# Two-phase blocks: a second MLP whose second products also go by Strassen's scheme

## The chip, the cores and the metric

The kernel runs on one core of a Trainium2 chip. The metric is the device time of one execution in microseconds (us); smaller is better. TensorE does the matmuls, VectorE (DVE) and ScalarE (ACT) work on elements, GpSimd (POOL) only issues the stores here, and SyncE (SP) only issues the loads. All transfers run on the core's 16 DMA engines.

## What is computed

A retention layer (a linear attention with decay) over q, k and v gives 3072 tokens of 512 features. Two MLPs follow, each with a hidden width of 2048:

```python
def _moe_ref(x, w_in, w_out):      # first MLP, "layer 0"
    h = x @ w_in
    g = np.maximum(0.01 * h, h)
    return (g @ w_out).astype(np.float32)

def _moe2_ref(x, w_in, w_out):     # second MLP, "layer 1"
    h = np.maximum(x @ w_in, 0.0)
    return (h * h @ w_out).astype(np.float32)
```

## The kernel before

Each MLP runs over three blocks of 1024 tokens (`b`), and a block has two halves of 512 tokens (`t`). Every matrix operand is split into a high and a low float32r part, and a product is three matmuls: high by high, low by high, high by low. The matmul is always 128x128 weights by 128x512 moving values. The hidden width is worked through in eight steps `q`, each with two 128-wide columns `j = 2q, 2q + 1`.

**First product.** In all blocks but the very first it goes by Strassen's scheme (in Winograd's form). For a step `q`, `emit_in` forms seven products of six matmuls, 42 in place of 48. Seven combinations of the weights ("units") are made once by `make_in` (`load_w`, `cast`, four subtractions, two splits), stored to DRAM (`wid`) and read again by `read_in`. Seven combinations of the tokens come from `operands` and lie in the tiles `xh1` to `xl7`.

**Second product.** It is plain: `emit_out` does 12 matmuls for one `j` and one half `t` (four output columns `m`, three passes). The weights come from `make_out` in the first block of a layer, which stores them to `wod`, and from `read_out` after that. A block has two passes. In the q loop the first product of step `q` alternates with `put_out` (second product, `t = 0`) of step `q - 1`; the hidden values of `t = 1` are kept in `t0` to `t7`. Then a second pass over the 16 `j` does the second product of `t = 1` in the order `LATE`: `split_late` splits the kept values, `read_out` brings the weights through the two buffers of the tile `wo`, and `operands` makes the next block's token combinations. So a block of layer 1 has 336 + 384 = 720 matmuls.

**Order.** Matmuls, loads and stores are kept in the order of the program. Loads form one queue on SP and stores one on POOL, and an issue that waits for its buffer holds back all behind it. ACT's and DVE's instructions are ordered when the program is built, by a planner that estimates when each becomes ready; on the chip each engine then goes strictly by that order.

**Work done ahead.** During the last block of layer 0 (`lay == 0`, `b == 2`), `make_in(1, 0, ..., True)` makes the first-product units of layer 1 for the steps in `AHEAD`, one after q = 1, 3, 5 and 7, through the tiles `ea` and `eb`. The others are made in layer 1's block 0, where raw weights come through the tile `sg` (`load_w`, 1 MiB each).

Of the kernel before, what the change touches and what calls it, by code (L numbers as in the profile page):

```python
# [9 lines left out]
F32 = mybir.dt.float32  # L10
F32R = mybir.dt.float32r
# [47 lines left out]
):  # L59
    nc = tc.nc  # L60
    x_p = ctx.enter_context(tc.tile_pool(name="x", bufs=1))
    w_p = ctx.enter_context(tc.tile_pool(name="w", bufs=1))
    g_p = ctx.enter_context(tc.tile_pool(name="g", bufs=2))
# [9 lines left out]

    def swap_pools():
        early.close()
        late["p"] = ctx.enter_context(tc.tile_pool(name="late", bufs=1))

    qt = const.tile([P, NP, C], F32, name="qt")
    vt = const.tile([P, NP, 2, 2], F32, name="vt")
# [10 lines left out]
    def store(**io):  # L90
        tc.keep_in_program_order(nc.gpsimd.dma_start(**io))
# [128 lines left out]


    wid = {}
    wod = {}
# [11 lines left out]
    stage = {}  # L235

    def load_w(lay, q, half):
        t = stage[lay, q, half] = w_p.tile([P, 1024], U64, tag="sg", name="sg", bufs=2)
        load(out=t, in_=src[lay][q, half])

    def cast(s, r):
# [71 lines left out]
    def get_in(lay, b, q):  # L313
        if lay == 0 and b == 0:
            plain_in(q)
        elif (lay == 0 and b == 1) or (lay == 1 and b == 0 and q not in AHEAD):
            make_in(lay, b, q)
        else:
            read_in(lay, b, q)

    def make_out(lay, q):
        load_w(lay, q, 1)
        if lay == 0 and 0 < q < NQ - 1:
            f = g_p.tile([P, 2, T], F32, tag=f"t{NQ - 1}", name="of", bufs=1).rearrange("p j c -> p (j c)")
        else:
            f = w_p.tile([P, 1024], F32, tag="wf", name="of", bufs=1)
        cast(stage.pop((lay, q, 1)), f)
        o = w_p.tile([P, 2, 2, 512], F32R, tag="wo", name="wo", bufs=2)
        fv = f.rearrange("p (j c) -> p j c", j=2)
        nc.scalar.copy(o[:, 0], fv)  # L330
        nc.vector.tensor_tensor(out=o[:, 1], in0=fv, in1=o[:, 0].bitcast(F32), op=ALU.subtract)
        store(out=wod[lay, q], in_=o.rearrange("p l j c -> p (l j c)").bitcast(F32))
        wout[lay, q] = o

    def read_out(lay, q):
        o = w_p.tile([P, 2, 2, 512], F32R, tag="wo", name="wo", bufs=2)
        load(out=o.rearrange("p l j c -> p (l j c)").bitcast(F32), in_=wod[lay, q])
        wout[lay, q] = o


# [47 lines left out]

    def keep(ps, t=None):
        if t is None:  # L390
            t = g_p.tile([P, T], F32, tag="g", name="g", bufs=3)
        nc.scalar.copy(t, ps)  # L392
        return t

# [9 lines left out]
    def emit_in(lay, b, q):  # L404

        j0, j1 = 2 * q, 2 * q + 1
        pa = ps_h.tile([P, T], F32, tag="h", name="pa")
        product(lay, b, q, 1, pa, True, True)
        c11 = g0[j0] = keep(pa)
        pd = ps_h.tile([P, T], F32, tag="h", name="pd")  # L410
        product(lay, b, q, 5, pd, True, True)
        late_g[q] = g_p.tile([P, 2, T], F32, tag=f"t{q}", name="g", bufs=1)
        c22 = g1[j1] = keep(pd, late_g[q][:, 1])
        yield
        product(lay, b, q, 6, pa, False, True)
# [15 lines left out]
        g = g0[j1] = g_p.tile([P, T], F32, tag="g", name="g", bufs=3)  # L431
# [12 lines left out]
    def emit_plain(q, i, t):  # L444
        j = 2 * q + i
        a = win[0, q]
        ps = ps_h.tile([P, T], F32, tag="h", name="pa")
        for kb in range(KB):
            kh, kt = divmod(kb, 2)
            unit = 2 * (1 - kh) + i if kh == 0 else 1 - i  # L450
            for k, (l, r) in enumerate(((0, 0), (1, 0), (0, 1))):
                mm(
                    out=ps, lhsT=a[:, l, unit, kt * P:(kt + 1) * P], rhs=xop[t, kh][r][:, kt],
                    start=kb == 0 and k == 0, stop=kb == KB - 1 and k == 2,
                )
        if t == 0:
            g = g_p.tile([P, T], F32, tag="g", name="g", bufs=3)
# [17 lines left out]
    def split_g(g, tag=None):  # L475
        if tag:
            gg = g_p.tile([P, 2, T], F32R, tag=tag, name="gg", bufs=1)
            gh, gl = gg[:, 0], gg[:, 1]
        else:
            gh = g_p.tile([P, T], F32R, tag="gh", name="gh")  # L480
            gl = g_p.tile([P, T], F32R, tag="gl", name="gl")
        mark[0] = nc.scalar.copy(gh, g).ins  # L482
        mark[1] = nc.vector.tensor_tensor(out=gl, in0=g, in1=gh.bitcast(F32), op=ALU.subtract).ins  # L483
        return gh, gl

    def emit_out(lay, b, t, j, part=(0, 12), begin=False, end=False):
# [10 lines left out]
        for k, m in order[part[0]:part[1]]:  # L497
            l, r = passes[k]
            mm(
                out=ac[m], lhsT=o[:, l, j % 2, m * P:(m + 1) * P], rhs=r,  # L500
                start=begin and k == 0, stop=end and k == 2,
            )
        if part[1] == 12:
# [18 lines left out]

    zero = g_p.tile([P, T], F32R, tag="gh", name="zero")
# [40 lines left out]

    for lay in range(2):
        for b in range(NB):
            last = lay == 1 and b == NB - 1
            if not last:  # L570
                nl, nb = (lay, b + 1) if b + 1 < NB else (1, 0)
            rest = (b + 2) * B * NP if lay == 0 and b + 1 < NB else 0
            for q in range(NQ):
# [11 lines left out]
                else:  # L585
# [12 lines left out]
                    for _ in part:  # L598
                        pass
                if q + 1 < NQ:  # L600
                    get_in(lay, b, q + 1)
                    get_out(lay, b, q + 1)
                elif not last:
                    get_in(nl, nb, 0)
                if not last and nl and q == 2:
# [12 lines left out]
            for i in range(NJ):  # L618
# [4 lines left out]
                    read_out(lay, LATE[i // 2 + 2])  # L623
                if rest and i < 9:
                    attend(rest)
                if not last:
# [5 lines left out]
                if not last and i == 13:  # L632
                    get_out(nl, nb, 0)
            evacuate(lay, b, 1)
            if (lay, b) == (0, NB - 2):
                swap_pools()


_OUT = ((NB, P, KB, TB), "float32")
# [62 lines left out]
```

## Time and profile before

| | |
|---|---|
| median of 3 runs | 1161.13 us (1159.62 to 1161.87) |
| the profiled execution: its own time | 1160.83 us |
| the profiled execution: its span, first to last instruction | 1158.8 us |
| TensorE busy | 1133.4 us (98%), 5402 matmuls |
| weight loads busy | 891.9 us (77%) |
| VectorE / ScalarE busy | 587.6 us (51%) / 508.2 us (44%) |
| granted TensorE clock, mean | 0.995 |

Times are microseconds from the first instruction. Matmul durations in the trace overlap, since matmuls are pipelined; the distance from one start to the next is the cost of one. Layer 0's last block runs from 484 to 659 us, layer 1's block 0 from there to 828, its block 1 to 991 and its block 2 to the end.

### The profile page before, as it was taken

The numbers are of one execution on the slowest core, as the hardware profiler recorded it, in microseconds if no ns is written. First come the engines' busy times: TensorE is split into PE (matmuls) and PEld (weight loads), VectorE is DVE, ScalarE is ACT, GpSimd is POOL, SyncE is SP. The second block draws the span as 40 slices with busy tenths as digits, with TensorE's granted clock in tenths as the row PEclk, the third lists the DMA queues.
The fourth block names the chain that finished last, engine by engine and source line by source line (L and its number), as shares of the span: only waits on it lengthen the run. The fifth ranks groups of instructions, "written<-read, shape, count | busy, mean of one in ns | idle before, by whom it ended". The sixth has DMA issues, their size and how long they took to land.

```text
span 1158.8 us, 13722 instructions
## 1 busy us (share of the span) xinstructions
PE 1133.4 (98%) x5402; PEld 891.9 (77%) x5402; DVE 587.6 (51%) x852; ACT 508.2 (44%) x793; POOL 54.2 (5%) x104
## 2 busy tenths in 40 slices
PE   8999999999999999999989999999999999999998
PEld 5677777767777776788867877788888888888886
DVE  5866555665444353442556477877232355233341
ACT  3755453323343342343445366755333353333431
POOL 0000000001000000000001000000000000000000
PEclk9999999999999999999999999999999999999999
DMA  9565654548455444749755788854746435645334
GB/s 373 234 245 201 234 202 150 186 140 291 184 211 218 167 169 164 254 191 371 300 200 209 300 314 321 318 198 181 297 158 258 184 143 195 239 197 200 136 126 165
DMA packets 48800, 255.71 MB, mean 221 GB/s; under 512 B 5984, under 2 KB 8032, under 8 KB 27872
## 3 DMA queue, kind: packets, MB, share of 16 engines
q1 hardware_dynamic: 36576, 192.04, 44.8%
q0 software_dynamic: 11584, 61.87, 13.5%
q8 instruction: 43, 0.70, 0.3%
q10 hardware_dynamic: 576, 0.93, 0.2%
q14 instruction: 21, 0.17, 0.0%
HBM read 191.90 MB, written 62.91 MB: 220 GB/s over the span
## 4 chain that ended last, share of the span: by engine, by line
PE 85%; DMA 9%; DVE 3%; ACT 2%; issue 1%; ACTq 0%; SPq 0%; DVEq 0%
PE acc L85 42%; PE pa L85 23%; PE pd L85 8%; DMA sg<-w 4%; PE y L85 4%; PE pb L85 4%; PE sc L85 3%; DMA wa<-wid 1%; DMA wo<-wod 1%; PE sp L85 1%; DMA gt<-gtab 1%; DVE of L248 1%; DMA wf<-wraw 1%; ACT sg L246 0%; DVE of L251 0%
## 5 line engine op out<-in xcount | busy, mean ns | idle before, releaser
L85 PE MATMUL acc<-gh,wo 128*128 128x512 f32 x1200 | 315.4, 394 | 9.8 <-ACT gh L482 6.0
L85 PEld LDWEIGHTS acc<-gh,wo 128*128 128x128 f32 x1200 | 225.5, 189 | 61.4 <-ACT gh L482 8.9
L85 PE MATMUL pa<-xh,wa 128*128 128x512 f32 x576 | 181.2, 395 | 2.3 <-DVE wa L272 1.4
L85 PE MATMUL acc<-gl,wo 128*128 128x512 f32 x600 | 169.3, 389 | 0.1
L483 DVE TENSOR_TENSOR gl<-g,gh 128x512 fp32r<-128x512 f32 x150 | 101.6, 688 | 77.6 <-PE acc L85 55.1
L85 PEld LDWEIGHTS acc<-gl,wo 128*128 128x128 f32 x600 | 112.6, 188 | 24.1 <-DVE gl L483 0.6
L85 PEld LDWEIGHTS pa<-xh,wa 128*128 128x128 f32 x576 | 106.2, 188 | 28.7 <-ACT g L462 2.3
L85 PE MATMUL acc<-gg,wo 128*128 128x512 f32 x504 | 122.1, 391 | 0.0
L482 ACT CAST gh<-g 128x512 fp32r<-128x512 f32 x150 | 91.2, 620 | 67.6 <-PE acc L85 66.8
L85 PE MATMUL pa<-xl,wa 128*128 128x512 f32 x288 | 112.5, 391 | 0.3 <-DVE xl L348 0.3
L85 PEld LDWEIGHTS acc<-gg,wo 128*128 128x128 f32 x504 | 94.0, 188 | 20.0 <-issue 0.7
L85 PE MATMUL pa<-xh,wb 128*128 128x512 f32 x320 | 99.6, 393 | 0.5 <-ACT g L392 0.5
L85 PE MATMUL pd<-xh,wa 128*128 128x512 f32 x320 | 98.7, 390 | 0.0
L418 DVE TENSOR_TENSOR g<-g,pd 128x512 f32<-128x512 f32 x40 | 27.5, 687 | 130.5 <-PE pd L85 122.7
L392 ACT COPY g<-pa 128x512 f32<-128x512 f32 x80 | 46.9, 587 | 98.5 <-PE pa L85 98.4
L85 PEld LDWEIGHTS pa<-xh,wb 128*128 128x128 f32 x320 | 59.4, 188 | 15.4 <-issue 1.7
L85 PEld LDWEIGHTS pd<-xh,wa 128*128 128x128 f32 x320 | 60.0, 188 | 12.7 <-ACT g L392 0.2
L149 DVE TENSOR_TENSOR pm<-sc,mk 128x384 f32<-128x384 f32 x96 | 49.2, 551 | 33.1 <-PE sc L85 30.8
L397 ACT ACTIVATE g<-g 128x512 f32<-128x512 f32 x48 | 30.2, 631 | 79.0 <-DVE g L422 31.8
L85 PEld LDWEIGHTS pa<-xl,wa 128*128 128x128 f32 x288 | 54.0, 188 | 12.3 <-DVE xl L348 0.7
L85 PE MATMUL pa<-xl,wb 128*128 128x512 f32 x160 | 62.3, 389 | 0.0
L85 PE MATMUL pd<-xl,wa 128*128 128x512 f32 x160 | 62.3, 389 | 0.0
(79 smaller groups left out, 1250.0 us busy)
## 6 DMA issues: line engine op xcount, KB each, us to landing
wo<-wod SPq DMA_DIRECT2D x68, 1024.0 KB, 4.8
sg<-w SPq DMA_DIRECT2D x32, 1024.0 KB, 7.7
wa<-wid SPq DMA_DIRECT2D x28, 1024.0 KB, 7.0
wb<-wid SPq DMA_DIRECT2D x28, 768.0 KB, 6.7
wod<-wo POOLq DMA_DIRECT2D x16, 1024.0 KB, 5.4
r<-first SPq DMA_DIRECT2D x48, 256.0 KB, 3.4
wid<-wa POOLq DMA_DIRECT2D x12, 1024.0 KB, 4.2
wid<-wb POOLq DMA_DIRECT2D x12, 768.0 KB, 5.7
```

What stands on the lines that cost most here:

```text
L85: tc.keep_in_program_order(nc.tensor.matmul(**kw))
L149: nc.vector.tensor_tensor(out=t, in0=sc[h][:, 128:512], in1=mk[:, p, h], op=ALU.mult)
L248: nc.vector.scalar_tensor_tensor(out=ru, in0=hi, scalar=0x80000000, in1=ru, op0=ALU.bitwise_and, op1=ALU.bitwise_or,)
L392: nc.scalar.copy(t, ps)
L397: nc.scalar.activation(out=g, in_=g, func=AF.Lrelu)
L418: nc.vector.tensor_tensor(out=c12, in0=c12, in1=pd, op=ALU.add)
L482: mark[0] = nc.scalar.copy(gh, g).ins
L483: mark[1] = nc.vector.tensor_tensor(out=gl, in0=g, in1=gh.bitcast(F32), op=ALU.subtract).ins
```

## The change

Layer 1's blocks 1 and 2 are taken out of the common loop and done by a new function, `both_block`, in two phases.

Phase 1 (`first_half`, `second_half`) forms the first products of all eight steps, the seven products of step `n` alternating with those of step `n - 1`. All hidden values are kept: `gu` (tiles `u0` to `u7`) and `gt_` (tiles `t0` to `t7`).

Phase 2 does the second product by the same scheme, with the hidden columns' parity, the output halves and the token halves as the two-by-two blocks. It has seven stages, in the order `STAGES`; each is one product over all eight `q` and two `m`, 48 matmuls, 336 in all. `prepare` forms and splits the next stage's hidden combination while a stage runs. `read_stage` reads a stage's weight units, four loads of 512 KiB, into tiles of the token combinations (or `t0` to `t7`) that are free by then.

The units of the second weights are eight in number and lie in one DRAM tensor per layer, `wou`: for each partition, unit, step, part and 256 columns. Units 0 to 3 are the plain quarters, written by `make_out` (also in layer 0, in place of `wod`); units 4 to 7 are made by the new `out_combinations` from a raw copy (`wraw`): for steps 0 and 1 in layer 1's block 0 during the pass for `t = 1`, for steps 2 to 7 in phase 1 of block 1. `read_out` now reads four pieces of 2 KiB per partition where it read 8 KiB in one.

Around this: weights and temporaries move to other memory pools, and layer 1's pool is exchanged for a new one (`swap_left`, `swap_right`) during its block 0; `AHEAD` has five steps, made after q = 0, 1, 2, 4 and 6; in layer 1's block 0 the raw weights are requested before `get_in`, every third through an additional `sg` buffer, and `read_x` comes at q = 4.

```diff
-AHEAD = (0, 1, 3, 5)
+AHEAD = {0: 0, 1: 1, 3: 2, 5: 4, 6: 6}
+OUNIT = {1: 0, 2: 2, 4: 3, 7: 4, 5: 5, 3: 6, 6: 7}
+STAGES = (1, 5, 6, 3, 7, 2, 4)
...
+    def swap_left():
+        mid.close()
+        late["p"] = ctx.enter_context(tc.tile_pool(name="units", bufs=1, reuse_waits="tile"))
...
-            wod[lay, q] = dram.tile([P, 2 * 1024], F32, name=f"wod{lay}_{q}")
+    wou = [dram.tile([P, 8 if lay else 4, NQ, 2, 256], F32, name=f"wou{lay}") for lay in range(2)]
...
+        pool, bufs = (late["p"], 1) if late and n_stage[0] % 3 == 0 else (w_p, 2)
+        t = stage[lay, q, half] = pool.tile([P, 1024], U64, tag="sg", name="sg", bufs=bufs)
...
-        store(out=wod[lay, q], in_=o.rearrange("p l j c -> p (l j c)").bitcast(F32))
+        put_units(lay, q, 0, o)
         wout[lay, q] = o
+        if lay:
+            store(out=wraw[q], in_=f)
+    def out_combinations(q, f, ta, tb):
+        load(out=f, in_=wraw[q])
+        yield
+        a11, a21, a12, a22 = (f[:, n * 256:n * 256 + 256] for n in range(4))
+        tt = nc.vector.tensor_tensor
+        tt(out=a11, in0=a11, in1=a21, op=ALU.subtract)
+        tt(out=a21, in0=a21, in1=a22, op=ALU.add)
+        tt(out=a22, in0=a22, in1=a11, op=ALU.subtract)
+        tt(out=a12, in0=a12, in1=a22, op=ALU.subtract)
+        for n, t in ((0, ta), (2, tb)):
+            u = t.bitcast(F32R).rearrange("p (n l c) -> p n l c", n=2, l=2)
+            h = f[:, n * 256:(n + 2) * 256].rearrange("p (n c) -> p n c", n=2)
+            nc.scalar.copy(u[:, :, 0], h)
+            nc.vector.tensor_tensor(out=u[:, :, 1], in0=h, in1=u[:, :, 0].bitcast(F32), op=ALU.subtract)
+            store(
+                out=wou[1][:, 4 + n:6 + n, q].rearrange("p n l c -> p n (l c)"),
+                in_=t.rearrange("p (n c) -> p n c", n=2),
+            )
     def read_out(lay, q):
+        load(
+            out=o.bitcast(F32).rearrange("p n l c -> p n (l c)"),
+            in_=wou[lay][:, 0:4, q].rearrange("p n l c -> p n (l c)"),
+        )
...
+    def read_stage(n, ks):
+        i = STAGES[n]
+        for k in ks:
...
+            load(out=t.bitcast(F32), in_=wou[1][:, OUNIT[i], 2 * k:2 * k + 2])
+            units[i, k] = t
+    def split_rot(i, q, s):
+        r = late["r"].tile([P, 2, T], F32R, tag="rot", name="rot", bufs=NQ)
+        mark[0] = nc.scalar.copy(r[:, 0], s).ins
+        mark[1] = nc.vector.tensor_tensor(out=r[:, 1], in0=s, in1=r[:, 0].bitcast(F32), op=ALU.subtract).ins
+        rot[i, q] = r
+    def first_half(b, q):
...
+        product(1, b, q, 1, pa, True, True)
+        nc.scalar.copy(u[:, 0], pa)
+        yield
+        product(1, b, q, 5, pd, True, True)
+        nc.scalar.copy(t[:, 1], pd)
+        yield
+        product(1, b, q, 6, pa, False, True)
+        nc.scalar.copy(t[:, 0], pa)
+        yield
+        product(1, b, q, 3, pd, False, True)
+        nc.vector.tensor_tensor(out=t[:, 0], in0=t[:, 0], in1=pd, op=ALU.add)
+        act_sbuf(1, t[:, 0], True)
+        yield pa
+    def second_half(b, q, pa):
...
+        product(1, b, q, 7, pa, False, True)
+        nc.vector.tensor_tensor(out=t[:, 1], in0=t[:, 1], in1=pa, op=ALU.add)
+        act_sbuf(1, t[:, 1], True)
+        yield
...
+        product(1, b, q, 2, pb, True, True)
+        nc.vector.tensor_tensor(out=u[:, 0], in0=u[:, 0], in1=pb, op=ALU.add)
+        act_sbuf(1, u[:, 0], False)
+        split_rot(1, q, u[:, 0])
+        nc.vector.tensor_tensor(out=u[:, 0], in0=t[:, 0], in1=u[:, 0], op=ALU.subtract)
+        nc.vector.tensor_tensor(out=t[:, 0], in0=t[:, 1], in1=t[:, 0], op=ALU.subtract)
+        yield
+        product(1, b, q, 4, pa, False, True)
+        nc.scalar.activation(out=u[:, 1], in_=pa, func=AF.Relu)
+        nc.vector.scalar_tensor_tensor(out=u[:, 1], in0=pa, scalar=0.0, in1=u[:, 1], op0=ALU.max, op1=ALU.mult)
+        yield
+    def prepare(i, q):
...
+        elif i == 6:
+            nc.vector.tensor_tensor(out=u[:, 0], in0=t[:, 1], in1=u[:, 0], op=ALU.subtract)
+            split_rot(i, q, u[:, 0])
...
+    def both_block(b):
...
+        for n in range(NQ + 1):
+            f = first_half(b, n) if n < NQ else iter(())
+            r = second_half(b, n - 1, pa) if n else iter(())
+            for k in range(4):
+                pa = next(f, None)
+                if n == NQ - 1 and k < 2:
+                    read_stage(0, (2 * k, 2 * k + 1))
+                if k < 3:
+                    next(r, None)
+            if n == NQ - 1:
+                read_stage(1, range(4))
+            if n and n + 1 < NQ:
+                read_units(b, n + 1)
...
+        for n, i in enumerate(STAGES):
...
+                if e % 2 and n + 1 < len(STAGES):
+                    prepare(STAGES[n + 1], q)
+                if e == 1:
+                    if 1 <= n <= 5:
+                        read_stage(n + 1, range(4))
+                    if n == 1 and not last:
+                        read_x(b + 1)
+                    if n in (3, 5) and not last:
+                        read_units(b + 1, (n - 3) // 2)
...
     for lay in range(2):
         for b in range(NB):
+            if lay and b:
+                both_block(b)
+                continue
...
+                    if lay:
+                        load_w(lay, q + 1, 1)
+                        if q + 1 not in AHEAD.values():
+                            load_w(lay, q + 1, 0)
...
-                if lay == 0 and b == NB - 1 and q % 2:
-                    make_in(1, 0, AHEAD[q // 2], True)
+                if lay == 0 and b == NB - 1 and q in AHEAD:
+                    make_in(1, 0, AHEAD[q], True)
...
+            if lay:
+                swap_left()
+                read_units(1, 0)
+                made = [out_combinations(e, *scratch(*(f"u{7 - 3 * e - k}" for k in range(3)))) for e in range(2)]
+                for m in made:
+                    next(m)
```

## Rows read from the trace of the kernel before

**Rows 1.** Stretches: us; busy (and instructions) of each engine; PE clock, DMA share, GB/s.

```profile
664.00:776.00 112.00, 109.28 (x473) 87.93 (x472) 89.20 (x117) 78.78 (x112) 10.53 (x20) 1.00 0.80 306
776.00:828.00 52.00, 52.00 (x230) 42.77 (x230) 27.53 (x34) 20.40 (x30) 3.33 (x7) 1.00 0.48 175
828.00:991.00 163.00, 163.00 (x720) 134.82 (x719) 63.56 (x87) 66.29 (x107) 4.05 (x8) 1.00 0.54 206
991.00:1154.50 163.50, 163.22 (x721) 134.73 (x719) 51.88 (x77) 59.65 (x100) 3.46 (x7) 1.00 0.46 174
```

**Rows 2.** The chain that ended last: start us, us, what.

```profile
827.68 1.36 PE pa L85 x6
...
991.00 1.36 PE pa L85 x6
...
1014.12 2.72 PE pa L85 x12
...
1154.26 0.69 DVE y L519
```

**Rows 3.** PE's waits, 460 to 830 us: total us, times, longest.

```profile
PE acc L85 <- ACT gh L482: 6.0, 5, 4.7
PE acc L85 <- DMA wo<-wod: 3.8, 2, 2.5
PE pa L85 <- DVE wa L272: 0.8, 1, 0.8
PE pa L85 <- DMA wa<-wid: 0.6, 1, 0.6
PE pa L85 <- ACT g L392: 0.5, 1, 0.5
```

**Rows 4.** The chain in layer 0's last block.

```profile
522.06 17.34 DMA wa<-wid
...
585.10 15.01 DMA sg<-w
...
604.36 12.52 PE acc L85 x48
...
616.89 7.82 DMA wo<-wod
...
624.84 34.23 PE acc L85 x144
```

**Rows 5.** The same columns as rows 1, around that place and two DMA-bound stretches.

```profile
524.50:539.50 15.00, 14.42 (x65) 11.62 (x63) 3.36 (x5) 5.76 (x12) 0.50 (x1) 1.00 1.01 399
585.00:604.40 19.40, 14.69 (x66) 11.86 (x64) 6.30 (x8) 8.51 (x15) 0.55 (x2) 0.98 0.69 269
604.40:606.90 2.50, 2.50 (x6) 2.02 (x7) 2.47 (x6) 1.16 (x2) 0.00 (x0) 0.50 0.00 0
690.00:705.00 15.00, 14.82 (x65) 11.93 (x65) 9.53 (x12) 8.82 (x13) 1.07 (x2) 1.00 1.01 416
```

**Rows 6.** Timelines of SP and ACT: start us, us, engine, line, operation.

```profile
521.63 0.38 SPq L88 DMA_DIRECT2D xs<-ydr  x1
522.06 0.42 SPq L88 DMA_DIRECT2D wa<-wid  x1
...
600.13 1.12 ACT L245 ACTIVATE wf<-sg 128x1024 f32<-128x1024 f32 x1 [5.82 <-DMA sg<-w]
...
789.40 33.19 SPq L88 DMA_DIRECT2D wo<-wod  x7
```

**Rows 7.** DMA issues: out<-in, engine, count, KB each, median us to landing.

```profile
wo<-wod SPq DMA_DIRECT2D x68, 1024.0 KB, 4.8
...
r<-first SPq DMA_DIRECT2D x48, 256.0 KB, 3.4
```

**Rows 8.** DVE and ACT groups: shapes, count, busy us, mean ns of one, idle before.

```profile
L483 DVE TENSOR_TENSOR gl<-g,gh 128x512 fp32r<-128x512 f32 x150 | 101.6, 688 | 77.6 <-PE acc L85 55.1 <-ACT gh L482 22.0
L418 DVE TENSOR_TENSOR g<-g,pd 128x512 f32<-128x512 f32 x40 | 27.5, 687 | 130.5 <-PE pd L85 122.7 <-ACT g L392 7.9
L402 DVE SCALAR_TENSOR_TENSOR g<-g 128x512 f32<-128x512 f32 x24 | 16.6, 690 | 0.7
L291 DVE TENSOR_TENSOR wf<-wf 128x256 f32<-128x256 f32 x16 | 6.8, 423 | 18.4 <-DMA wf<-wraw 18.3
L482 ACT CAST gh<-g 128x512 fp32r<-128x512 f32 x150 | 91.2, 620 | 67.6 <-PE acc L85 66.8 <-DVE g L436 0.4
L392 ACT COPY g<-pa 128x512 f32<-128x512 f32 x80 | 46.9, 587 | 98.5 <-PE pa L85 98.4
L399 ACT ACTIVATE g<-g 128x512 f32<-128x512 f32 x48 | 30.2, 630 | 49.3 <-DVE g L418 31.1 <-DVE g L422 18.1
```

More of the change, by code (lines that the diff above doesn't have):

```diff
@@ L234, in retention_then_two_mlps @@
     src = (w1, w2)
-    stage = {}
+    stage, n_stage = {}, [0]
     def load_w(lay, q, half):
-        t = stage[lay, q, half] = w_p.tile([P, 1024], U64, tag="sg", name="sg", bufs=2)
+        if (lay, q, half) in stage:
+            return
+        n_stage[0] += 1
+        pool, bufs = (late["p"], 1) if late and n_stage[0] % 3 == 0 else (w_p, 2)
+        t = stage[lay, q, half] = pool.tile([P, 1024], U64, tag="sg", name="sg", bufs=bufs)
         load(out=t, in_=src[lay][q, half])
@@ L315, in get_in @@
             plain_in(q)
-        elif (lay == 0 and b == 1) or (lay == 1 and b == 0 and q not in AHEAD):
+        elif (lay == 0 and b == 1) or (lay == 1 and b == 0 and q not in AHEAD.values()):
             make_in(lay, b, q)
@@ L324, in make_out @@
             f = g_p.tile([P, 2, T], F32, tag=f"t{NQ - 1}", name="of", bufs=1).rearrange("p j c -> p (j c)")
+        elif lay and q:
+            f = late["p"].tile([P, 1024], F32, tag=("ea", "eb")[q % 2], name="of")
         else:
@@ L327, in make_out @@
         cast(stage.pop((lay, q, 1)), f)
[L328 to L331, printed above, removed]
-        store(out=wod[lay, q], in_=o.rearrange("p l j c -> p (l j c)").bitcast(F32))
-        wout[lay, q] = o
-    def read_out(lay, q):
-        o = w_p.tile([P, 2, 2, 512], F32R, tag="wo", name="wo", bufs=2)
-        load(out=o.rearrange("p l j c -> p (l j c)").bitcast(F32), in_=wod[lay, q])
+        o = o_p.tile([P, 4, 2, 256], F32R, tag="wo", name="wo", bufs=2)
@@ new lines, in scratch, with put_units @@
+    def scratch(*tags):
+        out = []
+        for t in tags:
+            p = late["r"] if t == "ss" else g_p if t[0] == "t" else late["p"]
+            out.append(p.tile([P, 2, T], F32, tag=t, name="of", bufs=2 if t == "ss" else 1).rearrange("p i c -> p (i c)"))
+        return out
+    def put_units(lay, q, n, t):
+        store(
+            out=wou[lay][:, n:n + 4, q].rearrange("p n l c -> p n (l c)"),
+            in_=t.bitcast(F32).rearrange("p n l c -> p n (l c)"),
+        )
+    def read_out(lay, q):
+        o = o_p.tile([P, 4, 2, 256], F32R, tag="wo", name="wo", bufs=2)
+        load(
+            out=o.bitcast(F32).rearrange("p n l c -> p n (l c)"),
+            in_=wou[lay][:, 0:4, q].rearrange("p n l c -> p n (l c)"),
+        )
@@ L499, in emit_out @@
             mm(
-                out=ac[m], lhsT=o[:, l, j % 2, m * P:(m + 1) * P], rhs=r,
+                out=ac[m], lhsT=o[:, 2 * (j % 2) + m // 2, l, m % 2 * P:(m % 2 + 1) * P], rhs=r,
                 start=begin and k == 0, stop=end and k == 2,
@@ L521, in evacuate, with read_units @@
             put(out=dst[:, m, t * T:(t + 1) * T], in_=y)
-    zero = g_p.tile([P, T], F32R, tag="gh", name="zero")
+    gu, gt_, units, rot = {}, {}, {}, {}
+    def read_units(b, q):
+        a = late["p"].tile([P, 2, 4, 256], F32R, tag="wa", name="wa", bufs=2)
+        c = late["p"].tile([P, 2, 3, 256], F32R, tag="wb", name="wb", bufs=2)
+        load(out=a.rearrange("p l n c -> p (l n c)").bitcast(F32), in_=wid[1, q][:, 0:2048])
+        load(out=c.rearrange("p l n c -> p (l n c)").bitcast(F32), in_=wid[1, q][:, 2048:3584])
+        put_in(1, q, a, c)
@@ new lines, in split_rot @@
+    def split_rot(i, q, s):
[4 more added lines that the diff above has]
+    def first_half(b, q):
+        u = gu[q] = late["p"].tile([P, 2, T], F32, tag=f"u{q}", name="gu")
+        t = gt_[q] = g_p.tile([P, 2, T], F32, tag=f"t{q}", name="gt")
+        pa = ps_h.tile([P, T], F32, tag="h", name="pa")
+        pd = ps_acc.tile([P, T], F32, tag=f"acc{2 + q % 2}", name="pd")
+        product(1, b, q, 1, pa, True, True)
[11 more added lines that the diff above has]
+        yield pa
@@ new lines, in prepare @@
+    def prepare(i, q):
+        u, t = gu[q], gt_[q]
+        if i == 5:
+            split_rot(i, q, u[:, 0])
+        elif i == 6:
+            nc.vector.tensor_tensor(out=u[:, 0], in0=t[:, 1], in1=u[:, 0], op=ALU.subtract)
+            split_rot(i, q, u[:, 0])
+        elif i == 3:
+            split_rot(i, q, t[:, 1])
+        elif i == 7:
+            split_rot(i, q, t[:, 0])
+            nc.vector.tensor_tensor(out=u[:, 0], in0=u[:, 1], in1=u[:, 0], op=ALU.subtract)
+        elif i == 2:
+            split_rot(i, q, u[:, 1])
+        else:
+            split_rot(i, q, u[:, 0])
@@ new lines, in both_block @@
+    def both_block(b):
+        last = b == NB - 1
+        pa = made = None
+        for n in range(NQ + 1):
[11 more added lines that the diff above has]
+                read_units(b, n + 1)
+            if b == 1:
+                if n == 0:
+                    v = x_p.tile([P, KB, TB], F32, tag="xs", name="of").rearrange("p k (i c) -> p (k i) c", c=T)
+                    v = [v[:, 2 * e:2 * e + 2].rearrange("p i c -> p (i c)") for e in range(4)]
+                    near = [v[0:3], scratch("ss", "ss") + v[3:]]
+                if n:
+                    with tc.issue_after(mark[0]), tc.issue_after(mark[1]):
+                        next(made, None)
+                if n < 6:
+                    made = out_combinations(2 + n, *(scratch(*(f"{'ut'[n]}{e}" for e in (7, 6, 5))) if n < 2 else near[n % 2]))
+                    next(made)
+        A = [ps_acc.tile([P, T], F32, tag=f"acc{m}", name="acc") for m in range(2)]
+        s = {}
+        steps = None if last else operands(1, b + 1)
+        for n, i in enumerate(STAGES):
+            if i in (5, 2):
+                Dd = [ps_acc.tile([P, T], F32, tag=f"acc{2 + m}", name="acc") for m in range(2)]
+            bank = Dd if i in (5, 3, 2) else A
+            if i == 4:
+                order = [(q, m) for m in range(2) for q in range(NQ)]
+            else:
+                order = [(q, m) for q in range(NQ) for m in range(2)]
+            for e, (q, m) in enumerate(order):
+                r = rot[i, q]
+                for k, (l, h) in enumerate(((0, 0), (1, 0), (0, 1))):
+                    mm(
+                        out=bank[m], lhsT=units[i, q // 2][:, q % 2, l, m * P:(m + 1) * P], rhs=r[:, h],
+                        start=i in (1, 5, 2) and q == 0 and k == 0, stop=q == NQ - 1 and k == 2, skip_group_check=True,
+                    )
+                if e % 2 and n + 1 < len(STAGES):
[7 more added lines that the diff above has]
+                        read_units(b + 1, (n - 3) // 2)
+                if steps and e in {4: (7, 13), 5: (5, 11), 6: (1, 5, 9)}.get(n, ()):
+                    with tc.issue_after(mark[0]), tc.issue_after(mark[1]):
+                        next(steps, None)
+            if i in (1, 5):
+                s[i] = late["r"].tile([P, 2, T], F32, tag="ss", name="ss", bufs=2)
+            elif i == 6:
+                s[i] = x_p.tile([P, 2, T], F32, tag="xl4", name="ss")
+            elif i == 4:
+                s[i] = late["p"].tile([P, 2, T], F32, tag="u7", name="ss")
+            for m in range(2):
+                if i in (1, 5, 6) or (i == 4 and m == 0):
+                    nc.scalar.copy(s[i][:, m], bank[m])
+                elif i == 4:
+                    nc.vector.tensor_copy(s[i][:, m], bank[m])
+                else:
+                    y = s[{3: 6, 7: 5, 2: 1}[i]][:, m]
+                    nc.vector.tensor_tensor(out=y, in0=y, in1=bank[m], op=ALU.add)
+            if i in (3, 7, 2, 4):
+                y, mh, t = {3: (s.get(6), 0, 1), 7: (s.get(5), 1, 1), 2: (s.get(1), 0, 0), 4: (s.get(4), 1, 0)}[i]
+                for m in range(2):
+                    put = load if last and i == 4 else store
+                    put(out=out[b][:, 2 * mh + m, t * T:(t + 1) * T], in_=y[:, m])
@@ L625, in retention_then_two_mlps @@
                     attend(rest)
+                if lay and i in (4, 9):
+                    with tc.issue_after(mark[0]), tc.issue_after(mark[1]):
+                        next(made[i // 5], None)
+                if lay and i == 13:
+                    read_units(1, 1)
                 if not last:
@@ L631, in retention_then_two_mlps @@
                             next(steps, None)
-                if not last and i == 13:
+                if not lay and i == 13:
                     get_out(nl, nb, 0)
```

38 lines of the change are left out of this document (27 added, 11 removed).

## The prediction

> **What bounds the kernel now.** I first cut the last part of the span into stretches. In block 1 of layer 1 TensorE is busy for the whole stretch, in block 2 for all but 0.3 us; VectorE is busy for 64 and 52 us of 163, ScalarE for 66 and 60, and the DMA engines have a share of 0.54 and 0.46 [rows 1]. So these blocks are bound by matmuls alone. Their price comes from the chain of waits: the first product of block 1 starts at 827.68 and that of block 2 at 991.00 [rows 2], which is 163.32 us for 720 matmuls, 0.2268 us each; inside the block the chain shows 2.72 us for 12, the same [rows 2]. Nothing can be gained here by taking a wait away, only by taking matmuls away.
>
> Then I read TensorE's waits. After 830 us the view lists none. From 460 to 830 it lists 11.7 us, and two entries carry most of it: 4.7 us behind ScalarE's split `gh`, and 2.5 us for a read of `wo` [rows 3]. The chain puts both at the end of layer 0. A raw weight load `sg` takes from 585.10 to 600.11; ScalarE stands 5.82 us at its cast [rows 6] with two splits queued behind it, and matmuls resume at 604.36 [rows 4]. The read of `wo` issued at 616.89 lands after 7.82 us, and they resume at 624.84 [rows 4]. After the first idle stretch the granted clock is 0.50, that is 1.2 GHz in place of 2.4 [rows 5]; the 48 matmuls from 604.36 take 12.52 us in place of 10.88, the 144 from 624.84 take 34.23 in place of 32.65 [rows 4], so each stall costs another 1.6 us. Together the place costs 4.7 + 1.6 + 2.5 + 1.6 = 10.4 us.
>
> **What the change removes.** In each of two blocks the second product falls from 384 to 336 matmuls of the same shape: 2 x 48 x 0.2268 = 21.8 us. Since nothing waits in these blocks, this comes off in full if the new order keeps TensorE fed.
>
> **The end of layer 0.** `AHEAD` no longer makes units after q = 7. The load that ScalarE waited for stood behind two unit reads, with the stores of the preceding unit beside it (0.69 DMA share, 269 GB/s in 585 to 604 [rows 5]). The last one is now made after q = 6, and the one before it two steps earlier, so neither its load nor its stores meet the tail, and the stores of 1.8 MB that met the `wo` read of 616.89 are gone. I take the whole 10.4 us as saved; bounds 0 and 10.4.
>
> What is late next is the start of that block: q = 0, 1 and 2 now each make a unit. The stretch 524.5 to 539.5 already has a DMA share of 1.01 at 399 GB/s [rows 5], because `xs` of 2 MB goes out at 521.63; the `wa` behind it, issued at 522.06 [rows 6], takes 17.34 us [rows 4] and costs 0.6 [rows 3]. The change puts one more `sg` (1.05 MB) between them: 1.05 / 0.399 = 2.6 us later for the matmuls of q = 4. ScalarE's cast may again wait with copies queued behind it, up to the 5.8 of [rows 6]. I take +3.0; bounds 0 and 6.
>
> **Layer 1, block 0.** The other waits there sum to 1.3 us behind `gh`, 0.8 and 0.5 [rows 3], that is 2.6. Raw weights are now asked for before the unit reads, which should shorten them; against that stand 0.5 MB of raw copy per step at a mean DMA share of 0.80 and peaks of 1.01 with 416 GB/s [rows 1, 5]. I take 0; bounds -2.6 and +5.
>
> In its second pass seven `wo` reads go out in 33.19 us, 5.48 us apart [rows 6], and land in 4.8 [rows 7]: 0.7 us to spare. Two sets of new units now store 1.05 MB each in this pass, 2.6 us of the DMA engines at 399 GB/s, at most 2 x (2.6 - 0.7) = 3.8 us late. I take +2; bounds 0 and 3.8. The reads themselves now come in 2 KiB pieces in both layers. No row shows that for 1 MiB. From below it costs nothing; the 256 KB loads, which have 2 KB per partition, land in 3.4 us [rows 7], so four of them wholly in sequence would take 13.6. Since 256 KB and 1 MiB differ by only 1.4 us there, most of each is a fixed part that one larger issue pays once; I take +0.5 in all, and keep the upper end as the third rival.
>
> **Phase 1 of block 1.** One step is 42 matmuls, 9.52 us. VectorE has eight operations of 512 elements at 0.69 us [rows 8], 5.5 us, and in six steps the unit combinations: four of 256 at 0.42 and two of 512 at 0.69, 3.1 us; 8.6 of 9.52. ScalarE has three copies at 0.59, four activations at 0.63, a split at 0.62, one more activation at 0.60, and two splits for the units [rows 8], 6.8 us. Both fit, and where a product adds to a bank that an engine still has to read, 18 other matmuls (4.1 us) stand between, so a burst of 3.1 us is covered. The DMA engines must move 1.84 MB of units, 0.52 of raw weights and 1.05 of stores: 3.41 MB in 9.52 us is 358 GB/s, against 399 to 416 where the share is 1.01 [rows 5]. At 269 GB/s, the mixed stretch of [rows 5], a step would take 12.7 us, 3.2 too long, 19 over six steps. The saturated stretches also mix loads and stores, so I stay near them: +2; bounds 0 and 19. The unit reads need no short wait: `wa` of step n + 1 waits only for product 3 of step n - 1, a step ahead. In block 2 these additions are gone.
>
> **Phase 2.** A stage is 48 matmuls, 10.9 us. `prepare` costs VectorE 8 x 0.69 = 5.5 us, or 11.0 where a subtraction precedes the split (stages 6 and 7), and ScalarE 5.0 [rows 8]. The excess of 0.1 us is hidden, since each operand is made nearly a stage before its use. Weight units are 2.1 MB a stage, 193 GB/s; with `xs` beside them in one stage 4.2 MB, 385 GB/s. They are requested at a stage's start for the next one, and in quarters, so even a late last quarter has most of a further stage. I take +1 for both blocks' seams; bounds 0 and 5. The tail is unchanged: one copy of 0.69 us [rows 2] and one store.
>
> **Sum.** 1158.8 - 21.8 - 10.4 + 3.0 + 0 + 2 + 0.5 + 2 + 1 = 1135.1 us of span. The profiled execution took 1160.83, 2.0 more than its span, and the median of the runs is 0.3 above it: 1137.
>
> **Rivals.** First, block 1's first phase is bound by transfers or VectorE. For it speak 358 GB/s asked and 8.6 us of 9.52; against it the 18 matmuls of cover and 416 GB/s seen. Between the bounds, 11 us instead of 2: 1146, at the end 1154.
>
> Second, the 10.4 us at the end of layer 0 stay or form again elsewhere: the order on ScalarE is an estimate made beforehand, and a late load blocks it anywhere. Against it: of the earlier casts in that block none stalled TensorE at more than 0.6 us [rows 3]. 1147.
>
> Third, and slower: the second weights' reads land late, because `wou` spreads what was one 8 KiB run per partition over four pieces. Sixteen reads have no cover beyond 5.48 us (six in each pass without attention work, two at the ends of the other two). The gain of 24 us is gone at 1.5 us too much in each, a landing of 7.0 us; at the 7.8 of [rows 4] it is 16 x 2.3 = 37 us, 1174. Against it: 4.8 now, with only the piece size and the spacing changed. Page "DMA: Bandwidth & Descriptors" of the Trainium skill, section "Latency and other measured facts", speaks for it: rows of a DRAM tensor that lie large powers of two apart are read more slowly, 207 GB/s per direction at 512 KiB, 103 at 4 MiB, 214 with padding. Here the rows of `wou` lie 64 and 128 KiB apart and those of `wod` 8; no row of the trace shows such a spacing. By its nearest figure the loss would be 3% and this rival nothing; by its worst, half the rate, an estimate of 2.6 us more per read, it would be decided.
>
> **Chances.** The forecast 0.65, with its own range of 1126 (no new loss, and the 2.6 us gone too) to 1145; the first rival 0.14, the second 0.10, the third 0.11. About 0.2% is what a measurement of this kernel can tell from no change. Faster: the first three but for 0.02 where two rivals meet, 0.87; the third rival gives 0.08 of slower and 0.03 within 0.2%, which with those 0.02 split is 0.09 and 0.04. The range 1126 to 1152 leaves out the third rival and the first one's end.
>
> **What would show it.** Right: blocks 1 and 2 start 153 to 157 us apart with TensorE busy throughout; 96 matmuls fewer; no wait above 1 us between 585 and 630; `wo` landing near 5 us. Wrong: waits of TensorE for `wa`, `wb` or `wu` in phases 1 and 2, a DMA share of 1 there, matmuls waiting for `rot`, or a `wo` wait at every second `j` of a second pass.

## The result

The changed kernel takes 1178.24 us (median of 4 runs, 1175.13 to 1182.22) against 1161.5 for the kernel before on the same chip: a ratio of 1.0143, 95% interval 1.0101 to 1.0185. It is slower; 1137 was forecast. The profiled execution is the slowest run, with a span of 1180.4 us against 1158.8. Of all runs told below one, of `a_align` (1180.41 us), was in a slower state of the chip and is left out of that kernel's median and ratio.

**Where the time went.** From the page of the kernel after, the engines:

```profile
PE 1133.4 (96%) x5306; PEld 875.3 (74%) x5306; DVE 676.9 (57%) x1018; ACT 546.1 (46%) x863; POOL 75.9 (6%) x130
```

The 96 matmuls are gone, yet TensorE is busy as long as before, 1133.4 us: the rest have become longer. Its chain that ended last (start us, us, what), from the end of layer 0:

```profile
592.24 10.41 DMA sg<-w
...
640.93 5.90 DMA wo<-wou
...
652.77 5.75 DMA wo<-wou
...
670.19 8.37 DMA wo<-wou
...
698.00 15.99 DMA sg<-w
...
732.75 14.26 DMA sg<-w
...
866.66 1.39 PE pa L99 x6
...
943.63 78.39 PE acc L99 x336
...
1022.03 1.39 PE pa L99 x6
...
1098.21 78.42 PE acc L99 x336
```

Against [rows 2 and 4]: block 1 of layer 1 starts at 866.66 instead of 827.68, 39 us late before the two new blocks begin. Block 1 takes 155.4 us instead of 163.32 and block 2 154.6, where 152.4 were due (672 x 0.2268). A second phase is one unbroken run of 336 matmuls at 0.2333 us. The windows of the first three of the four phases (columns of [rows 1]) and TensorE's waits (total us, times, longest):

```profile
866.60:943.60 77.00, 76.53 (x338) 62.96 (x337) 53.75 (x97) 46.64 (x82) 9.90 (x15) 1.00 0.85 310
943.60:1022.00 78.40, 78.40 (x338) 63.07 (x337) 60.13 (x86) 41.20 (x64) 3.81 (x7) 1.00 0.67 249
1022.00:1098.20 76.20, 76.20 (x338) 63.10 (x337) 39.98 (x61) 39.90 (x70) 0.54 (x1) 1.00 0.59 203
```

```profile
PE acc L99 <- DMA wo<-wou: 8.4, 8, 2.9
PE pa L99 <- ACT g L446: 8.3, 5, 2.1
PE acc L99 <- ACT gh L536: 6.5, 5, 2.3
PE sc L99 <- DVE g L472: 4.9, 6, 1.9
```

In phase 2 TensorE is busy for all of 78.40 us at a granted clock of 1.00: neither a wait nor the clock makes its matmuls long. The waits are for reads of `wo`, which were 3.8 us [rows 3], and behind ScalarE and VectorE, which also unpack the weights that loads bring. The DMA issues (KB each, median us to landing):

```profile
wo<-wou SPq DMA_DIRECT2D x40, 1024.0 KB, 6.3
sg<-w SPq DMA_DIRECT2D x32, 1024.0 KB, 10.3
...
wf<-wraw SPq DMA_DIRECT2D x8, 512.0 KB, 7.7
```

`wo` landed in 4.8 before [rows 7]. Stage by stage, from first matmul to first matmul of the next stage (us); "both repairs" is a kernel told below:

| stage | before | forecast | after | both repairs |
|---|---|---|---|---|
| layer 0, blocks 0 and 1 | 446.7 | 0 | +16.0 | +0.4 |
| layer 0, block 2 | 174.6 | -7.4 | +10.8 | -5.9 |
| layer 1, block 0, q loop | 124.9 | 0 | +9.6 | +8.8 |
| its second pass | 43.8 | +2 | +2.4 | +1.6 |
| blocks 1 and 2 | 331.3 | -18.8 | -17.3 | -20.3 |

(The forecast's +0.5 for pieces had no stage of its own.)

### The profile page after: what moved, and what is told of

It reads as the page before. It is cut to its first block, busy times and chain, and to the rows that moved or that the text cites. A ratio compares the mean times of both kernels' runs of the same rounds, so it can differ in the third digit from the quotient of the medians.

```text
span 1180.4 us, 14047 instructions
## 1 busy us (share of the span) xinstructions
PE 1133.4 (96%) x5306; PEld 875.3 (74%) x5306; DVE 676.9 (57%) x1018; ACT 546.1 (46%) x863; POOL 75.9 (6%) x130
## 4 chain that ended last, share of the span: by engine, by line
PE 72%; DMA 19%; DVE 4%; ACT 3%; issue 1%; SPq 0%; ACTq 0%; DVEq 0%
PE acc L99 36%; PE pa L99 20%; DMA sg<-w 8%; PE pd L99 6%; DMA wf<-wraw 4%; DMA wo<-wou 4%; PE y L99 4%; PE pb L99 3%; PE sc L99 3%; DMA wa<-wid 2%; PE sp L99 1%; ACT wf L262 1%; DMA gt<-gtab 1%; ACT sg L263 1%; DVE g L472 1%
## 5 line engine op out<-in xcount | busy, mean ns | idle before, releaser
L99 PE MATMUL acc<-gh,wo 128*128 128x512 f32 x800 | 215.8, 401 | 15.0 <-DMA wo<-wou 8.4
L99 PEld LDWEIGHTS acc<-gh,wo 128*128 128x128 f32 x800 | 150.2, 191 | 55.7 <-ACT gh L536 10.3
L99 PE MATMUL acc<-rot,wu 128*128 128x512 f32 x672 | 157.1, 395 | 0.0
L99 PEld LDWEIGHTS acc<-rot,wu 128*128 128x128 f32 x672 | 126.1, 188 | 30.6
L99 PE MATMUL acc<-gl,wo 128*128 128x512 f32 x400 | 115.0, 395 | 1.4 <-DVE gl L537 1.4
L537 DVE TENSOR_TENSOR gl<-g,gh 128x512 fp32r<-128x512 f32 x100 | 67.6, 688 | 46.2 <-PE acc L99 33.0
L99 PEld LDWEIGHTS acc<-gl,wo 128*128 128x128 f32 x400 | 75.8, 190 | 20.0 <-DVE gl L537 3.5
L99 PE MATMUL acc<-gg,wo 128*128 128x512 f32 x336 | 83.8, 398 | 0.0
L602 DVE TENSOR_TENSOR rot<-gu,rot 128x512 fp32r<-128x512 f32 x80 | 54.7, 688 | 26.8 <-ACT rot L601 26.5
L601 ACT CAST rot<-gu 128x512 fp32r<-128x512 f32 x80 | 49.7, 621 | 42.1 <-PE acc L99 36.8
```

Of the source, the lines that this page charges most:

```text
L99: tc.keep_in_program_order(nc.tensor.matmul(**kw))
L601: mark[0] = nc.scalar.copy(r[:, 0], s).ins
L602: mark[1] = nc.vector.tensor_tensor(out=r[:, 1], in0=s, in1=r[:, 0].bitcast(F32), op=ALU.subtract).ins
```

## The experiments

**Two theories for the 39 us lost ahead of the new blocks and the long matmuls inside them.** One: the 2 KiB pieces of `wou`. Two: the place of the moved tiles. The pools that the change opens on the right-hand side of the memory end at its upper edge, so that in the built kernel `wo`, `gh`, `gl`, `g` and `rot` start 96 bytes beyond a multiple of 128; before, all operands of the two MLPs' matmuls start on one. Each is repaired alone, then both; and each is put alone into the kernel before.

`a_align`: 96 bytes ahead of the right-hand pools.

```diff
+    edge = ctx.enter_context(tc.tile_pool(name="edge", bufs=1, side="right"))
+    edge.tile([P, 24], F32, name="edge")
```

> The changed kernel with 96 bytes left free at the right-hand edge of the memory, so that every tile of the right-hand pools (wo, gh, gl, g, rot) starts at a multiple of 128 bytes; as changed they start 96 bytes past one. Placement theory: the steps from matmul to matmul of 231 to 238 ns go back to 227, 11 us over the program, and wo lands in 4.8 us again, so that stalls of 10 to 20 us go too: 1150 to 1160. Piece theory (the 2 KiB pieces of wou slow its reads): at most the 11 us of steps, wo still near 5.9 where nothing else moves: 1165 to 1170. If neither steps nor landings move, placement is out: 1178.

`a_runs`: the units of one step side by side, so that `read_out` reads one 8 KiB run per partition again (the stages of phase 2 then read two pieces of 2 KiB); the rows stay 64 KiB apart in layer 0 and 128 in layer 1.

```diff
-    wou = [dram.tile([P, 8 if lay else 4, NQ, 2, 256], F32, ...
+    wou = [dram.tile([P, NQ, 8 if lay else 4, 2, 256], F32, ...
```

> The changed kernel with the unit tensor laid out step by step, so that read_out and make_out move 8 KiB per partition in one run again (the stages of phase 2 then read two pieces of 2 KiB in place of one of 4). Piece theory: wo lands in 4.8 us, the stalls before layer 1's block 1 shrink by 20 to 30 us, steps stay at 231 to 238: 1148 to 1158. Placement theory: wo stays near 5.9 us and the time within 4 us of 1178. Order theory (the new list of units made ahead and the new order of loads cost the time by themselves): layer 0's block 1 is as slow as in the changed kernel.

`a_both`: the two together.

> Both repairs on the changed kernel: the 96 bytes at the right-hand edge and the unit tensor laid out step by step. If the two causes are separate, the steps fall from 231 to 238 back to 227 ns in all blocks, which is 10.7 us of excess counted in the trace of the version with 8 KiB runs (1154.3): 1143 to 1145. If placement had worked mainly through the transfers, which are already repaired, less: 1148 to 1154.

`b_right`: the kernel before, its `wo`, `g`, `gh` and `gl` in a right-hand pool. `b_pieces`: the kernel before, its second weights in `wou`.

> The kernel before, with only wo, gh, gl and g moved to a pool on the right side, as the change does, starting 96 bytes past a multiple of 128. Placement theory: steps of 229 to 236 ns in the second products, some 8 to 12 us more, and wo landing later than 4.8: 1170 to 1190. Piece theory: landings and time as before, 1161, but for steps.

> The kernel before, with only the second weights' DRAM copy laid out in four pieces of 2 KiB per partition, 64 KiB per partition apart in all, as the change does. Piece theory: wo lands near 5.9 us, the attention block and the second passes stall: 1175 to 1195. Placement theory: wo near 4.8 to 5.0, 1161 to 1163.

| kernel | median us | ratio (95%) |
|---|---|---|
| a_align | 1168.06 | 1.0072 (1.0029 to 1.0115) |
| a_runs | 1154.29 | 0.9947 (0.9929 to 0.9964) |
| a_both | 1143.94 | 0.984 (0.9813 to 0.9867) |
| b_right | 1172.23 | 1.0091 (1.0072 to 1.0109) |
| b_pieces | 1195.57 | 1.0307 (1.0274 to 1.034) |

Both are real, and within the noise they add: by the medians 24.0 us for the pieces alone, 10.2 for the place alone, 34.3 together. The 10.2 is uncertain, since the runs of `a_align` spread from 1161.85 to 1178.49 (by the ratios it is 8, with intervals that overlap). The place is clear of noise where the pieces are out of the way: 10.4 from `a_runs` to `a_both`, and 10.6 in `b_right`. `wo` still lands in 6.2 us in `a_align` and in 4.8 in `b_right`, so the place of the tiles is not what makes the reads late. A phase 2 in the chains of `a_runs` and of `a_both`, which differ in the 96 bytes alone:

```profile
914.09 78.41 PE acc L99 x336
```

```profile
911.27 76.17 PE acc L101 x336
```

The second is 0.2267 us a matmul, the price of before. In `b_pieces` TensorE waits for `wo` 18 times, 16.8 us, where it waited 3.8. Its span is 34.9 us longer: TensorE is idle for 47.8 us in place of 25.4, and busy 12.5 us longer with the same matmuls, in part because they run at a granted clock of 0.50 after some of the waits.

**Pieces, or the distance between them?** `e_planes`: the kernel before with 2 KiB pieces, but the rows of a piece 2 KiB apart.

> The kernel before with the second weights' DRAM copy in pieces of 2 KiB whose rows lie 2 KiB apart (four planes of 256 KiB per step) instead of 64 KiB apart. The version with 64 KiB between rows took 1195.6, wo landing at 6.3 us. If the size of the piece is the cause: as slow, 1190 to 1200. If the spacing of the rows is: wo at 4.8 to 5.0 and 1161 to 1165.

1168.42 us, 1.006 (1.0041 to 1.0079): 7 us instead of 34, a miss for both ranges. The issues of `wo` on SP's queue (duration ns, least, median, most) and their landing, for the kernel before, `a_runs`, `e_planes` and `b_pieces`:

```profile
L88 SPq DMA_DIRECT2D wo<-wod x68: 319/320/327, 214.7 to 1143.4; - x68
DMA to landing us min/median/max: 4.1/4.8/11.2
```

```profile
L102 SPq DMA_DIRECT2D wo<-wou x40: 319/320/327, 213.2 to 824.8; - x40
DMA to landing us min/median/max: 4.1/4.8/17.9
```

```profile
L88 SPq DMA_DIRECT2D wo<-wou x68: 359/371/382, 212.4 to 1147.9; - x68
DMA to landing us min/median/max: 4.7/5.6/14.1
```

```profile
L88 SPq DMA_DIRECT2D wo<-wou x68: 518/529/612, 212.6 to 1177.3; - x68
DMA to landing us min/median/max: 4.6/6.3/13.9
```

Neither far rows alone (`a_runs`: 4.8 us) nor small pieces alone (5.6) explain 6.3; it takes both. Why they act together no run shows; SP's longer issue is only 0.2 us of the 1.5.

**How far off may a tile be?** `e_edge64`: `a_both` with 32 bytes of padding, so that the tiles start 64 beyond a multiple of 128.

> The version with both repairs, with 32 bytes free at the right-hand edge instead of 96, so that the right-hand tiles start 64 bytes past a multiple of 128. If a multiple of 64 is enough, steps of 227 ns and 1144 as with 96; if 128 is needed, steps of 231 to 238 and 1152 to 1156.

1150.3 us, 0.9914 (0.9887 to 0.9942): 6.4 us slower than `a_both`, a miss for both ranges. A phase 2 lies between the two:

```profile
912.89 76.92 PE acc L101 x336
```

In phase 2 only the moving values `rot` lie on the right-hand side: 226.7 ns from start to start in `a_both`, 228.9 here, 233.3 as changed. Matmuls of which only the weights `wo` lie there (their moving values are the kept tiles of the second pass) take 233.3 ns already at 64, as against 227.6 in `a_both`.

**Is the end of layer 0 what was forecast?** `c_ahead`: `a_both` with the old places, `AHEAD = {1: 0, 3: 1, 5: 3, 7: 5}`.

> The version with both repairs, with the old list of units made ahead (four, after q = 1, 3, 5 and 7). If the step of the prediction on the end of layer 0 is right, the stalls of 4.7 and 2.5 us behind the late raw weight and the late read come back with the low clock behind them, 5 to 10 us in layer 0's last block; block 0 of layer 1 then has one unit more to make. Slower than the version with both repairs by 5 to 12 us. If that place was not worth its 10 us, within 3.

1153.59 us, 0.9923 (0.99 to 0.9947): 9.6 more than `a_both`, 5.9 of it in that block. Its waits show the old one again, as in [rows 3], and one of 2.6 us for a read of `wo` behind it:

```profile
PE acc L101 <- ACT gh L538: 4.7, 2, 4.5
```

**The 9 us in layer 1's block 0.** `a_both` still has them (133.7 us for the q loop, where its 528 matmuls at 0.2267 us would take 119.7), and its chain has loads of `sg` in the place of waits:

```profile
664.91 15.21 DMA sg<-w
...
698.74 15.53 DMA sg<-w
```

Suspects: the raw copies (`wraw`), the new order of the requests, the third `sg` buffer. `c_noraw` drops the stores of the copies, `c_order` restores the order (the lines below), `d_sg` gives `sg` two buffers of one pool, `e_order_sg` joins the last two.

```diff
-                    if lay:
-                        load_w(lay, q + 1, 1)
-                        if q + 1 not in AHEAD.values():
-                            load_w(lay, q + 1, 0)
```

> The version with both repairs, without the raw copies of the second weights that layer 1's block 0 stores (0.5 MB a step); the combinations made from them then use layer 0's copies. Its q loop in block 0 takes 9 us longer than in the kernel before. Transfer theory: the copies fill a stretch in which the DMA engines are already full, weight loads land earlier without them and 4 to 9 us come off: 1135 to 1140 against 1144. Order theory (the raw weights are asked for too early and ScalarE's casts stand in front of the copies from the banks): within 2 us of the version with both repairs.

> The version with both repairs, but layer 1's block 0 asks for the raw weights where the kernel before does, after the unit reads. Order theory: the q loop of that block falls from 134 to about 125 us and the time by 5 to 9 us. Transfer theory: no gain, since the same bytes move; the casts may even start later, 1144 to 1150.

> The version with both repairs with two sg buffers instead of three. Buffer theory: raw loads go out later, casts are ordered later, the q loop of block 0 falls by 3 to 9 us from 133.7. Reading theory: no change, or slower by up to 5 since loads start later.

> The version with both repairs, old request order and two sg buffers, unpacking in ea and eb, copies kept: the combination not yet tried. If the order in which ScalarE gets the casts sets the 9 us and the three places to put data only shift it, 1140 to 1146 with stalls in other places; if early requests and the third buffer have to go together, the q loop falls to 125 to 129 us and the time to 1135 to 1139.

The medians are 1142.68, 1144.69, 1142.63 and 1142.33, the q loop 131.9, 134.9, 133.2 and 133.8: none brings the 9 us back by itself, nor do the last two together. So the block was brought back to the old kernel's way as a whole. `d_wf` only unpacks in `wf` again instead of `ea` and `eb`; `d_plain` has `wf`, the old order and two `sg` buffers; `d_plainx` also `read_x` at its old place.

```diff
-        elif lay and q:
-            f = late["p"].tile([P, 1024], F32, tag=("ea", "eb")[q % 2], name="of")
```

> The version with both repairs; in layer 1's block 0 the raw second weights are unpacked in the tile wf again, which the first weights use too, instead of in ea and eb. Left to explain are 9 us in that block's q loop (133.7 us against 124.9 in the kernel before), which neither the copies nor the request order account for. Buffer theory: more places to put raw weights let the casts be ordered early on ScalarE, where they stand waiting for late loads in front of the bank copies; with one place fewer the loop falls by 3 to 9 us. Reading theory (the later read_x and the mix of units cause it): no change.

> The version with both repairs with all three particulars of layer 1's block 0 taken back (request order, wf, two sg buffers); what stays new there are the raw copies, the list of units and read_x at q = 4. Buffer theory: the q loop is back at 125 to 128 us, 6 to 9 off, 1136 to 1139. Reading theory: still 132 to 136, 1142 to 1146.

> The same with read_x at q = 2 as in the kernel before. Reading theory: only now is the loop back at 125 to 128 us. Buffer theory: like the version before it, within 2 us.

They take 1181.54, 1178.17 and 1175.07: a miss for every theory, with the q loop at 165.7 to 171.5 us. `d_plain`'s waits from 640 to 840 us show what holds it:

```profile
PE pa L101 <- ACT wa L288: 37.9, 3, 16.7
...
ACT wf L262 <- DMA wraw<-of: 11.1, 2, 6.6
```

The store of a raw copy reads `wf`, and into the same tile the weights of the next first-product units `wa` are unpacked: ScalarE waits for that store (two of them stand in the chain with 10.9 and 14.3 us from issue to landing), and TensorE for `wa`. `e_plain_noraw` takes the store out of `d_plain`.

> The version with both repairs whose layer 1 block 0 has the old request order, two sg buffers and wf, now also without the raw copies of the second weights (layer 0's are used for the combinations). With the copies its q loop took 167.7 us, because the next unpacking waits until the copy has left wf. If that tile held by its store is what the copies cost, the loop is back at 125 to 128 us and the time at 1133 to 1138. If the list of units or the later read_x costs the 9 us, 132 to 136 and 1141 to 1145.

1132.09 us, 0.975 (0.9728 to 0.9772); the q loop takes 122.8, 2.1 less than before the change. The stores of the raw copies are what holds `d_plain`, then, but this run takes away their 4.2 MB too. It also differs from `c_noraw` (131.9) in nothing but the order, the buffers and `wf`: without the copies, the three together cost 9 us. `f_pool` keeps them and lets go of the tile: GpSimd copies it to `ea` or `eb`, and the store reads that. `g_copy` is `f_pool` without the store.

```diff
+            r = late["p"].tile([P, 1024], F32, tag=("ea", "eb")[q % 2], name="of")
+            nc.gpsimd.tensor_copy(out=r, in_=f)
-            store(out=wraw[q], in_=f)
+            store(out=wraw[q], in_=r)
```

> Towards a version that keeps the gain: both repairs, layer 1's block 0 with old request order, two sg buffers and wf, the raw copy kept, but GpSimd, which stands idle, first copies wf into ea or eb and the store goes out from there. Without any raw copies this version took 1132.1 with a q loop of 122.8 us; with the store straight from wf 1178.2 and 167.7 us. If what the copies cost is the time that their store holds wf, the loop is back at 123 to 128 us: 1132 to 1140. If the copy on GpSimd itself holds wf long or disturbs VectorE, or the bytes matter after all, 1142 or more.

> The version with GpSimd's copy of the raw weights, but the copy is not stored in layer 1 (left out: the combinations use layer 0's raw copies of the same steps). Block 0's eight steps took 131.0 us with copy and store and 122.8 with neither. If the stores' 4.2 MB among saturated transfers cost the difference, 122 to 125 us there and 1131 to 1134 in all; if GpSimd's copy holds the unpack tile too long, 129 to 131 and 1138 to 1140.

`f_pool`: 1139.68 us, 0.9808 (0.9795 to 0.9822), the fastest of the kernels that do the whole work; the time is in the first range, the q loop of 131.0 is not. `g_copy`: 1132.06, 0.9753 (0.9729 to 0.9777), as expected of the stores. Their windows over that q loop, `f_pool` first:

```profile
653.00:784.00 131.00, 124.39 (x530) 101.06 (x529) 90.34 (x117) 82.26 (x118) 23.88 (x36) 0.97 0.81 308
```

```profile
650.00:772.00 122.00, 120.24 (x530) 98.91 (x529) 91.64 (x118) 82.26 (x119) 18.83 (x26) 1.00 0.81 302
```

The same rate of transfer in both, 308 and 302 GB/s, and 3.5 MB less to move in the second (131 x 308 against 122 x 302). GpSimd's copies, 1.2 us each, cost nothing (`g_copy` against `e_plain_noraw`). The tile held by its store cost 37 us (`d_plain` against `f_pool`), and the stores themselves cost 9: TensorE is idle for 6.6 us in place of 1.8, and busy for 124.4 in place of 120.2, at a granted clock of 0.97 in place of 1.00. The bytes would explain it (3.5 MB at 308 GB/s are 11 us), but no run separates them from the place of these stores in the queue.

## Why the prediction was wrong

**What failed.** The step "I take +0.5 in all, and keep the upper end as the third rival" for the reads in 2 KiB pieces, together with that rival's chance of 0.11. Repaired alone it gives back 24.0 us, with the other repair in place 24.1 by the medians and 26.9 by the ratios. The bound was drawn from 256 KB loads of 2 KB per partition, whose rows say nothing of distance. The rival had the cause right, and the place only in part. At a landing of 6.3, under its 7.0, the gain was gone. Between the profiled executions of the changed kernel and of `a_runs` lie 13.8 us in layer 0's blocks 0 and 1, where the rival had four reads, and 15.9 in its block 2, of which 6.4 are in the second pass, where it had six. In the second pass of layer 1's block 0, where it had the other six, `a_runs` gains nothing: `wo` lands in 6.5 us there even in 8 KiB runs, with rows 128 KiB apart and the new units' stores beside it. Of the 41 us between 1137 and 1178.24, this step is 24 to 27; most of the rest are the next two.

The Trainium skill, page "DMA: Bandwidth & Descriptors", section "Latency and other measured facts", gives rates for rows from 512 KiB apart on: 207 GB/s there against 214 at full rate, which makes a loss of 3%, an estimate from these figures. By it, the forecast said, this rival would be nothing. No run here has rows 512 KiB apart. At 64 KiB they show no loss in 8 KiB runs (`a_runs`, 4.8 us) and a loss in 2 KiB pieces, of which that section says nothing: 6.3 us for 4.8 (`b_pieces`).

**What was missing.** No term asked where the moved pools place their tiles, though the text of the change said that they move: 10.4 us once the pieces are repaired, 10.6 in `b_right`. "2 x 48 x 0.2268" took the step of a matmul as fixed; in phase 2 it was 0.2333, 2.2 us a phase.

**Layer 1, block 0.** "I take 0", bounds -2.6 and +5; it was +9.6, and +8.8 with both repairs. The forecast counted the raw copies' 0.5 MB per step and let the earlier requests pay for them. Two things each hold this q loop at 131 to 134 us: the stores of the copies, with the order, the buffers and the unpacking tile as before (`f_pool`, 131.0), and the new order, buffers and unpacking tiles together, without any store (`c_noraw`, 131.9). Only without both is it 122 to 123 (`e_plain_noraw`, `g_copy`), which is why taking one away gave back 1.8 us at most. Which of the three particulars counts stays open.

**What held.** The -21.8 and +2 and +1, which make -18.8: with aligned tiles blocks 1 and 2 are 20.3 us shorter (phase 1 of block 1 +2.3, phase 2 none, phase 1 of block 2 none). The first rival did not come: 0.85 DMA share, 310 GB/s, and 0.5 us of idle TensorE. Of its own signs, blocks 1 and 2 start 155.4 us apart and 96 matmuls are gone, as said; `wo` landing near 5 us failed. The end of layer 0: the second pass of that block is 43.5 us with both repairs, and from 580 us to its end no wait above 0.5 us is left; the sum of -10.4 and +3.0 was forecast as -7.4 and is -5.9. One slip there: the text ahead says that units are made after q = 0, 1, 2, 4 and 6, but the dictionary puts them after 0, 1, 3, 5 and 6 (0, 1, 2, 4 and 6 are the steps whose units are made). So the load at q = 2 that the +3.0 was worked out from is at q = 3, the one before the last is made one step later than said, and that the sum came so near is partly luck. Second pass of layer 1's block 0: +2 forecast, +1.6. So the change itself was worth what was said: with both repairs the span is 1143.6 us, and of its 8.5 above the 1135.1 of the sum block 0 alone is 8.8.

## What to carry to other kernels

When a change lays a DRAM tensor out anew, cost its reads by the run that one partition reads and by the distance between rows together, and try the layout alone in the old kernel first. When tiles change pools, look at their start addresses in the built program before trusting an old matmul's price. A store that reads a working tile holds that tile until it has landed, 10.9 and 14.3 us in `d_plain`: give it a copy of its own, and still count the store where the DMA engines are busy (a share of 0.81 here). When taking back one part at a time gains nothing, take all back and put them in again one by one: two causes can each hold the same place.

## What was not expected of the hardware

- The step of a 128x128 by 128x512 float32r matmul depends on where its operands start: 226.7 ns in phase 2 with all of them on multiples of 128 bytes. With the moving values alone off it, it was 228.9 at 64 bytes beyond one (`e_edge64`) and 233.3 at 96 (the changed kernel, 670 steps each); with the weights alone off it, 233.3 at 64 and 233.6 at 96 (300 steps each). With both 96 beyond it was 230.7 (`gh`) and 228.1 (`gl`), less than with one. These are means of the steps under 260 ns from start to start; no run shows why.
- A 1 MiB read took 4.8 us in 8 KiB runs with rows 64 KiB apart, 5.6 in 2 KiB pieces with rows 2 KiB apart, and 6.3 in 2 KiB pieces with far rows; its issue took SP 320, 371 and 529 ns (all medians).
